# Moving TensorE's semaphore waits out of the 64x64 tile matmuls, onto full 128x128 products of the step before

## The chip, the cores and the metric

The kernel runs on one core of one Trainium2 chip. The metric is the time of one execution on the device in microseconds (us), the median of several runs. The core has five engines, each with its own instruction stream that runs in order: TensorE (PE, matmuls; its weight loads are shown apart as PEld), VectorE (DVE), ScalarE (ACT), GpSimd (POOL) and SyncE (SP, which issues the DMAs). The streams are tied to each other by semaphores: an instruction can wait until a semaphore that another engine raises has reached a value.

## The reference, cut to what matters

A layer norm, then two branches from its result: sliding-window attention with 32 heads of 20 columns and a window of 256 keys, and an MLP with a squared ReLU. The two are multiplied, with a SiLU on the MLP's side, and added to the input. S is 2048, D is 640, F is 1536.

```python
x = A_x
xn = _layernorm(x, axis=-1)
s = _A_ref(xn, A_wqkv, A_wo)
g = _silu(_B_ref(xn, B_w1, B_b1, B_w2, B_b2))
return x + s * g
```

`_A_ref` is `softmax(mask(q @ k.T * Dh**-0.5)) @ v`, the mask keeping keys 0 to 255 behind each query, followed by `@ wo`; `_B_ref` is `relu(xn @ w1 + b1)**2 @ w2 + b2`.

## The kernel before

All big products are done in float16 with operands split into a high and a low part, so one product in the reference becomes three on the chip. After a first part (layer norm, values, the first group of queries and keys, up to about 120 us of the profile) comes one long loop of 269 steps, the loop `for s in range(steps)` at L1023, in which attention and all the remaining dense products are interleaved by hand: the code is written in the order in which each engine is to run it, and no scheduler moves anything. A pair of heads (there are 16) takes 16 steps, one for each tile of 128 queries.

In step s, PE does this, in this order:

1. In every fourth step (s % 4 == 1) a transpose (`max_rows`, L584) of row maxima that POOL wrote to `mp`.
2. `scores` (L558): four matmuls into `sps`, each on a 64x64 quarter of the array, for the two heads of the pair. They are read by `maxima` on DVE (L569), which finds the row maxima. `sps` are two PSUM banks.
3. `scores_t` (L605): four more such quarter matmuls into `stps`, the transposed scores of ten steps earlier (LAG is 10), with the maxima already in two extra rows of `qs` (so in `scores_t` a wait for the small DMAs that bring those rows). `stps` is one tile. It is read by the exponential on ACT (`exps`, L610).
4. `fill` (L1007): full 128x128 products of the rest of the network, drawn from a generator in two portions, L1066 and L1075. Their lines are L689 (`mm_group`: queries and keys `qkps`, hidden units `hps`, and at the end `wops`) and L874 (`out_unit`, `yps`). Between the portions come the DVE and ACT parts that empty finished banks.
5. In every second step (s even, from 14 on) `values` (L638): 24 or fewer short full products into `ops` that multiply the exponentials of two query tiles with the values. In these steps the second portion of `fill` is 0.3 us smaller, in the others 0.3 us larger (SWING).

Steps with `values` are called value steps below, the others plain steps. Items 2 and 3 together are the "stretch of tiles": eight matmuls on quarters of the array, between full products on both sides. There are 266 such stretches: 256 steps have `scores`, and `scores_t` goes on for ten more.

On ACT the order in a step is: the exponential (L610), then the relu and square of a hidden unit if one is finished (L848, L849), then the float16 copy of the exponential of the step before (`high`, L618). DVE does the two maxima (L569), in every fourth step a copy of the transposed maxima (`mrow`, L588), the low part of an older exponential (L624), and what empties PSUM banks.

Who must wait for whom in a stretch: `scores` may overwrite `sps` only when DVE has read the maxima of the step before; `scores_t` may overwrite `stps` only when ACT has done the exponential of the step before; both need the DMAs that load `qs` and `ks`. These waits sit on the instruction that needs them, so inside the stretch.

Of the kernel before, what the change touches and what calls it, by code (L numbers as in the profile page):

```python
# [14 lines left out]
P = 128  # L15
# [42 lines left out]
def attn_mlp_kernel(ctx: ExitStack, tc, x, wqkv, wo, w1, b1, w2, b2, out):  # L58
# [485 lines left out]
        vps[p] = vp  # L544

    mts = {}

    def scores(p, q, between):
        i = p % 2
        r = [pat.tile([P, 4 * P], F32, tag="s", name="sps") for h in range(2)]  # L550
        rows = between and between(r[0])
        nk = min(WIN + HB, (q + 1) * P)
        for j in range(2):
            q0 = q * P + j * HB
            k0 = max(0, q0 - WIN)
            for h, ps in enumerate(r):
                rows_ = slice(HB * h, HB * h + HR)
                nc.tensor.matmul(ps[HB * j:HB * (j + 1), :nk], qs[i][rows_, q0:q0 + HB], ks[i][rows_, k0:k0 + nk], start=True, stop=True)  # L558
        return (r, mask if q > 1 else mask0[:, 2 * P - nk:], nk), rows

    def maxima(p, q, r):
        if q % 4 == 0:
            mts[p, q // 4] = mtp_.tile([P, 8], F32, tag="mt", name="mt")
        mt = mts[p, q // 4]
        r, mk, nk = r
        for h, ps in enumerate(r):
            junk = mtp_.tile([P, WIN + HB], BF16, tag="junk", name="junk")
            at_ = 4 * h + q % 4
            nc.vector.tensor_tensor_reduce(out=junk[:, :nk], in0=ps[:, :nk], in1=mk, scale=1.0 / MAX_UNIT, scalar=-3.0e38, op0=ALU.add, op1=ALU.max, accum_out=mt[:, at_:at_ + 1])  # L569
        if q % 4 == 3:  # L570
            mp = mps[q // 4 % 2]
            v = mp[:, 0:16].rearrange("p (h a b) -> p h a b", h=2, a=2)
            m_ = mt.rearrange("p (h b) -> p h b", h=2)
            nc.gpsimd.tensor_copy(v[:, :, 0, :], m_)  # L574
            nc.gpsimd.tensor_sub(v[:, :, 1, :], m_, v[:, :, 0, :])
            mts[p, q // 4] = mp

    def max_rows(p, g, tp=None):
        i = p % 2
        mp = mts.pop((p, g))  # L580
        if tp is None:
            tp = pat.tile([P, 4 * P], F32, tag="s", name="mtp")
        tp = tp[:, 3 * P:3 * P + P // 2].bitcast(F16)
        nc.tensor.transpose(tp, mp, identh)  # L584

        def rest():
            mrow = mtp_.tile([16, P], F16, tag="mrow", name="mrow")
            nc.vector.tensor_copy(mrow, tp[0:16, :])  # L588
            for h in range(2):
                post(qs[i][HB * h + HR:HB * h + ER, 4 * P * g:4 * P * (g + 1)].rearrange("a (b n) -> a b n", n=P), mrow[8 * h:8 * (h + 1), :])  # L590
        return rest

    pts = {}
    ots = {}
    sts = []

    def scores_t(p, kb):
        i = p % 2
# [8 lines left out]

    def exps(p, kb, ps, n):
        p32 = at2.tile([P, 2, 3 * P], F32, tag="p32", bufs=3, name="p32")
        nc.scalar.activation(p32[:, :, :n], ps[:, :, :n], AF.Exp, scale=esc[0], bias=ebias)  # L610
# [50 lines left out]
    state = [0.0, 0.0, 0]  # L661
    posts = []

    def post(dst, src):
        posts.append((dst, src))

    def post_all():
        for dst, src in posts:
            nc.sync.dma_start(dst, src)
        posts.clear()  # L670

    pending, late = [], []
# [5 lines left out]
    def flush(upto=None):  # L678
# [3 lines left out]
        while pending and (upto is None or flushed[0] < upto):  # L682
            flushed[0] += 1
            pending.pop(0)()

    def mm_group(ps, mms, cost):
        n = len(mms)
        for j, (a, b_) in enumerate(mms):
            nc.tensor.matmul(ps, a, b_, start=j == 0, stop=j == n - 1)  # L689
            yield cost  # L690


    bulk = []
# [8 lines left out]
            fn()  # L702
            credit[0] -= cost

    def bulk_dma(cost, dst, src):
        item = (cost, lambda: nc.sync.dma_start(dst, src))
        bulk.append(item)
        return item

# [148 lines left out]
    def out_unit(n, tt, nh, third):  # L858
        if (n, tt, nh, third) == (0, 0, 0, 0):
            for j in range(3):  # L860
                ensure(f"2{j}")
        t = n * 2 + tt
        sl = slice(nh * HALF, (nh + 1) * HALF)
        fs = range(third * THIRD, (third + 1) * THIRD)
        flush(ready_h[n, fs[-1]])
        if third == 0:
            if nh == 0:
                outs[t] = wgt.tile([P, D], F32, tag="ysb", name="ysb")
            outs[t, nh] = pmm.tile([P, HALF], F32, tag="mm", name="yps")
        ps, ysb = outs[t, nh], outs[t]  # L870
        for fc in fs:
            hh = hidden[n, fc // 2][:, fc % 2]
            for j, (hp, wp) in enumerate(((0, 0), (0, 1), (1, 0))):
                nc.tensor.matmul(ps, hh[:, hp, tt * P:(tt + 1) * P], lin1(w2t, (2 * fc + wp) * D + nh * HALF, HALF), start=fc == 0 and j == 0, stop=fc == NF - 1 and j == 2)  # L874
                yield 0.138

        def evac():
            nc.vector.scalar_tensor_tensor(ysb[:, sl], ps, mlp["i2"], b2t[:, sl], ALU.mult, ALU.add)
# [138 lines left out]
    with tc.manual_schedule(engines={E_.PE, E_.Activation, E_.DVE, E_.Pool, E_.SP}):  # L1017
# [5 lines left out]
        for s in range(steps):  # L1023
            state[2] = s
            post_all()
            issue(RATE)
            a, b, c, d, e = (at_step(s - lag) for lag in (0, LAG, LAG + 1, LAG + 2, LAG + 3))
            if a:
                p, q = a
                if q == 0:  # L1030
                    ensure_bulk(loads)
                if s == 2:
                    ones_rows(1)
                if s == 3:
                    nc.scalar.activation(early, eps, AF.Exp)
                    sts.append(pst.tile([P, 2, 4 * P], F32, tag="st", name="stps"))
                    nc.vector.memset(sts[0][:, :, 0:3 * P], 0.0)
                if s == 5:
                    load_v(0)
                if q == 2 and p < NP - 1:  # L1040
                    loads = [bulk_dma(0.7, *l) for l in pair_loads(p + 1, 0)]
                if q == LAG and p < NP - 1:
                    loads += [bulk_dma(0.7, *l) for l in pair_loads(p + 1, 1)]
                if q == LAG + 4 and p < NP - 1:
                    load_v(p + 1)
            rows = between = None
            if s % 4 == 1 and 1 < s <= NP * NT + 1:
                def between(tp=None, s=s):
                    return max_rows((s - 2) // NT, (s - 2) % NT // 4, tp)
# [62 lines left out]
```

## Time and profile before

| | |
|---|---|
| median of 3 runs | 838.02 us (837.1 to 838.42) |
| the profiled execution's own time | 837.25 us |
| its span, first to last instruction | 835.5 us |
| busy: PE, DVE, ACT, POOL | 98%, 82%, 78%, 57% of the span |
| mean granted clock of PE | 0.998 of full speed |
| the loop with stretches of tiles | about 120 to 750 us of the span |

How to read the rows shown below. A row of the timeline has the start in us from the span's start, the length in us, engine, source line, operation, output and inputs, shapes, how many equal ones that follow each other are merged (x8), and in brackets the idle time of the engine ahead of it with what ended it. Matmuls overlap in the pipeline: a product of 128x320 is listed with a length of 0.30 us, but the next one starts 0.136 us later. A row of the groups has the count, the busy time in all, the mean length of one in ns, and the idle time ahead. A row of the windows has, for each engine, the busy time within the stretch of time named at its start.

### The profile page before, as it was taken

Reading aid. Unit: us, or ns where it says so; the run is one execution under the profiler, and the core shown is the slowest. Engines: PE = TensorE matmul, PEld = TensorE weight load, DVE = VectorE, ACT = ScalarE, POOL = GpSimd, SP = SyncE. Lnnn points to the kernel's source line nnn. Section 1 sums busy time; section 2 is a strip of 40 time slices with the busy share of each in tenths; the row PEclk is TensorE's granted clock in tenths of the full one; section 3 lists DMA queues with packets and bytes.
Section 4 is the critical chain, followed back from the end, with each engine's and each line's share of the span. In section 5 each row is a group of like instructions: output and inputs, shape, how many; then the busy total and the mean of one; then the engine's idle time right before and its main releaser. Section 6 shows DMA issues by size and latency. Waiting matters only on the chain.

```text
span 835.5 us, 24908 instructions
## 1 busy us (share of the span) xinstructions
PE 815.3 (98%) x9426; PEld 548.1 (66%) x9426; DVE 686.0 (82%) x1897; ACT 648.5 (78%) x1028; POOL 476.9 (57%) x874
## 2 busy tenths in 40 slices
PE   8999999999989999999999999999999999999998
PEld 6765563445545557777777777777777777767775
DVE  6777576788999889888988889888988889875665
ACT  5456455998898989898898989898898989893321
POOL 2000001446777768797878878797887878770000
PEclk9999999999999999999999999999999999999999
DMA  6894447765463332212121212211121131055873
GB/s 240 253 342 123 146 147 255 232 183 158 145 197 119 100 102 79 52 49 66 50 68 58 67 49 54 56 60 50 54 89 45 55 97 46 10 199 181 309 288 129
DMA packets 100497, 104.51 MB, mean 125 GB/s; under 512 B 42520, under 2 KB 72856, under 8 KB 100376
## 3 DMA queue, kind: packets, MB, share of 16 engines
q1 hardware_dynamic: 100376, 102.91, 39.5%
q8 instruction: 74, 1.21, 0.6%
q14 instruction: 47, 0.39, 0.2%
HBM read 65.67 MB, written 36.83 MB: 123 GB/s over the span
## 4 chain that ended last, share of the span: by engine, by line
PE 82%; ACT 7%; DVE 5%; issue 3%; DMA 2%; SPq 0%; DVEq 0%; ACTq 0%
PE hps L689 19%; PE yps L874 19%; PE wops L689 8%; PE ops L638 7%; PE vps L292 7%; PE sps L558 7%; PE qkps L689 7%; PE stps L605 3%; PE qkps L503 3%; ACT p L610 2%; DVE junk L569 2%; ACT ph L618 1%; PE otp L956 1%; PE tps L256 1%; DVE pl L624 1%
## 5 line engine op out<-in xcount | busy, mean ns | idle before, releaser
L610 ACT ACTIVATE p<-stps,ebias,esc 128x768 f32<-128x768 f32 (+2 forms) x256 | 242.3, 947 | 50.2 <-PE stps L605 42.4
L569 DVE CUSTOM_DVE_ANT_0 junk<-sps,mask 128x320 bf16<-128x320 f32 (+2 forms) x512 | 221.3, 469 | 54.8 <-PE sps L558 44.6
L624 DVE TENSOR_TENSOR pl<-p,ph 128x768 f16<-128x768 f32 (+2 forms) x256 | 243.6, 952 | 4.7 <-ACT ph L618 4.0
L611 POOL TENSOR_SCALAR_AFFINE_SELECT p<-p 128x256 f32<-128x256 f32 x256 | 171.4, 670 | 90.4 <-ACT p L610 87.8
L618 ACT ACTIVATE ph<-p 128x768 f16<-128x768 f32 (+2 forms) x256 | 203.2, 794 | 1.9 <-POOL p L613 0.9
L689 PE MATMUL hps<-xT,w 128*128 128x256 f16 x1440 | 188.8, 273 | 0.0
L874 PE MATMUL yps<-w,hh 128*128 128x320 f16 x1152 | 186.6, 300 | 0.0
L689 PEld LDWEIGHTS <-w 128*128 128x128 f16 x1440 | 133.3, 98 | 43.7 <-issue 23.7
L874 PEld LDWEIGHTS <-hh 128*128 128x128 f16 x1152 | 105.1, 98 | 55.6 <-issue 21.8
L689 PE MATMUL qkps<-xT,qkw 128*128 128x512 f16 x480 | 117.0, 381 | 0.8 <-DVE w_t L153 0.8
L613 POOL TENSOR_SCALAR_AFFINE_SELECT p<-p 128x256 f32<-128x256 f32 x224 | 110.5, 493 | 0.0
L558 PE MATMUL sps<-ks,qs 60*64 60x320 f16 (+2 forms) x1024 | 86.1, 313 | 6.5 <-DVE mt L569 5.9
L638 PE MATMUL ops<-vp,ph 128*128 128x41 f16 x1440 | 89.8, 181 | 0.0
L638 PE MATMUL ops<-vp,pl 128*128 128x41 f16 x1440 | 89.5, 181 | 0.0
L638 PEld LDWEIGHTS <-ph 128*128 128x128 f16 x1440 | 84.6, 96 | 6.2 <-issue 0.6
L638 PEld LDWEIGHTS <-pl 128*128 128x128 f16 x1440 | 78.9, 96 | 5.8
L605 PE MATMUL stps<-qs,ks 62*64 62x320 f16 (+4 forms) x1024 | 79.6, 291 | 2.3 <-ACT p L610 2.0
L574 POOL CAST mp<-mt 128x8 f16<-128x8 f32 x64 | 44.1, 689 | 62.2 <-DVE mt L569 61.6
L689 PEld LDWEIGHTS <-qkw 128*128 128x128 f16 x480 | 41.6, 98 | 53.4 <-issue 11.7
L852 POOL TENSOR_TENSOR hh<-sq,hh 128x256 f16<-128x256 f32 x96 | 67.6, 704 | 13.0 <-DVE sq L851 9.3
L292 PE MATMUL vps<-wv,xT 128*128 128x320 f16 x480 | 70.0, 302 | 3.2 <-ACT xT L261 1.6
L689 PE MATMUL wops<-wo,oT 128*128 128x320 f16 x480 | 66.7, 299 | 0.8 <-ACT oT L121 0.8
(150 smaller groups left out, 974.8 us busy)
## 6 DMA issues: line engine op xcount, KB each, us to landing
ks<-k_d SPq DMA_DIRECT2D x64, 120.0 KB
qs<-q_d SPq DMA_DIRECT2D x64, 120.0 KB
raw<-in_B_w_dram SPq DMA_DIRECT2D x24, 320.0 KB
v_d<-vt SPq DMA_DIRECT2D x8, 656.0 KB
vp<-v_d SPq DMA_DIRECT2D x16, 328.0 KB
xt<-in_A_x_dram SPq DMA_DIRECT2D x16, 320.0 KB
k_d<-shm SPq DMA_DIRECT2D x20, 256.0 KB
q_d<-shm SPq DMA_DIRECT2D x20, 256.0 KB
```

Source lines behind the costliest of these rows:

```text
L292: nc.tensor.matmul(ps, xT[b][:, xp, c, t * P:(t + 1) * P], wv[wp][:, c, nh * HALF:(nh + 1) * HALF], start=n == 0, stop=n == 3 * KC - 1)
L558: nc.tensor.matmul(ps[HB * j:HB * (j + 1), :nk], qs[i][rows_, q0:q0 + HB], ks[i][rows_, k0:k0 + nk], start=True, stop=True)
L569: nc.vector.tensor_tensor_reduce(out=junk[:, :nk], in0=ps[:, :nk], in1=mk, scale=1.0 / MAX_UNIT, scalar=-3.0e38, op0=ALU.add, op1=ALU.max, ...
L605: nc.tensor.matmul(ps[HB * j:HB * (j + 1), hh, c0:c1], ks[i][rows_, kb * P + HB * j:kb * P + HB * (j + 1)], qs[i][rows_, kb * P + c0:kb * ...
L610: nc.scalar.activation(p32[:, :, :n], ps[:, :, :n], AF.Exp, scale=esc[0], bias=ebias)
L611: nc.gpsimd.affine_select(p32[:, :, 0:P], p32[:, :, 0:P], pattern=[[0, 2], [1, P]], compare_op=ALU.is_ge, fill=0.0, base=0, channel_multip ...
L613: nc.gpsimd.affine_select(p32[:, :, 2 * P:], p32[:, :, 2 * P:], pattern=[[0, 2], [-1, P]], compare_op=ALU.is_gt, fill=0.0, base=0, channel ...
L618: nc.scalar.activation(ph[:, :, :n], p32[:, :, :n], AF.Copy)
L624: nc.vector.tensor_sub(pl[:, :, :n], p32[:, :, :n], ph[:, :, :n])
L638: nc.tensor.matmul(ot[:, q % 4, hh, :], t[:, hh, (q - k) * P:(q - k + 1) * P], vp[:, k // 4, k % 4, hh, :], start=m == 1, stop=m == 2 * le ...
L689: nc.tensor.matmul(ps, a, b_, start=j == 0, stop=j == n - 1)
L874: nc.tensor.matmul(ps, hh[:, hp, tt * P:(tt + 1) * P], lin1(w2t, (2 * fc + wp) * D + nh * HALF, HALF), start=fc == 0 and j == 0, stop=fc = ...
```

## The change

The scores' two PSUM banks and the bank of the sums are made once (`sps`, `opst`) rather than asked of the pool in each step. Each instruction that reads a bank of a stretch (the last of the two maxima, the `mrow` copy, the exponential), and each POOL write or DMA that the next stretch needs, is noted in a list `users`. At the end of the fill of step s, ahead of `values`, `wait_ahead` gives the last full products of that step a wait for them, one each, from the last product backwards: the last product waits for the maxima of this step, the one before it for `mrow` in the steps that have one, the next for this step's exponential, and those before for POOL writes and DMAs that the next step needs. A wait that PE has already done isn't repeated, so the stretch of the next step has none left. DMAs are issued by the new helper `send` in the same order.

```diff
     def scores(p, q, between):
         i = p % 2
-        r = [pat.tile([P, 4 * P], F32, tag="s", name="sps") for h in range(2)]
-        rows = between and between(r[0])
+        if not sps:
+            sps.extend(pat.tile([P, 4 * P], F32, tag="s", name="sps") for h in range(2))
+        r = sps
+        rows = between and between()
...
+            read = nc.vector.tensor_tensor_reduce(out=junk[:, :nk], in0=ps[:, :nk], in1=mk, scale=1.0 / MAX_UNIT, scalar=-3.0e38, op0=ALU.add, op1=ALU.max, accum_out=mt[:, at_:at_ + 1])
+        users.append(read)
...
+            landing.append((p * NT + q + 2, nc.gpsimd.tensor_sub(v[:, :, 1, :], m_, v[:, :, 0, :])))
...
+            users.append(nc.vector.tensor_copy(mrow, tp[0:16, :]))
...
-        nc.scalar.activation(p32[:, :, :n], ps[:, :, :n], AF.Exp, scale=esc[0], bias=ebias)
+        users.append(nc.scalar.activation(p32[:, :, :n], ps[:, :, :n], AF.Exp, scale=esc[0], bias=ebias))
...
-            ots[p, q // 4] = po_.tile([P, 4, 2, VW], F32, tag="o", name="ops")
+            if not opst:
+                opst.append(po_.tile([P, 4, 2, VW], F32, tag="o", name="ops"))
+            ots[p, q // 4] = opst[0]
...
+    def send(dst, src, due=0):
+        dma = nc.sync.dma_start(dst, src)
+        if due:
+            landing.append((due, dma))
...
+    dense = []
+
     def mm_group(ps, mms, cost):
         n = len(mms)
         for j, (a, b_) in enumerate(mms):
-            nc.tensor.matmul(ps, a, b_, start=j == 0, stop=j == n - 1)
+            dense.append(nc.tensor.matmul(ps, a, b_, start=j == 0, stop=j == n - 1))
             yield cost
+
+    def wait_ahead(s):
+        for item in landing[:]:
+            if item[0] <= s + 1:
+                users.append(item[1])
+                landing.remove(item)
+        for mm, user in zip(reversed(dense), users):
+            tc.add_manual_dep(mm.ins, user.ins.name, mybir.DependencyInfo(mybir.DependencyClass.Sync, mybir.DependencyReason.DATA))
+        dense.clear()
+        users.clear()
...
             fill((1 - EARLY_FILL) * per + SWING * (-1) ** (s - LAG - 3))
+            wait_ahead(s)
             if e and e[1] % 2:
                 values(e[0], e[1] - 1)
```

The order of instructions is the same on all five engines; only PE's waits differ. Two places of PE's stream show it, both around step 116, a value step (its stretch starts at 401.86 us in the profile of before). Names in brackets are the semaphores waited for: DVE and Activation are raised by those engines, DMAHW by landing DMAs, Pool by POOL.

The first place is the stretch itself. Before, on PE, from its first weight load on:

```order
L558 LDWEIGHTS qs1_1562
L558 MATMUL sps_7388<-ks1_1563,qs1_1562 64x320 [waits DVE_49]
L558 LDWEIGHTS qs1_1562
L558 MATMUL sps_7389<-ks1_1563,qs1_1562 64x320 [waits DVE_49]
L558 LDWEIGHTS qs1_1562
L558 MATMUL sps_7388<-ks1_1563,qs1_1562 64x320
L558 LDWEIGHTS qs1_1562
L558 MATMUL sps_7389<-ks1_1563,qs1_1562 64x320
L605 LDWEIGHTS ks0_127 [waits DMAHW7_49]
L605 MATMUL stps_1647<-qs0_126,ks0_127 64x320 [waits Activation_49]
```

Now, on PE, the last four full products ahead of the same stretch, and its first load:

```order
L896 LDWEIGHTS hh_6169 [waits DMAHW0_49]
L896 MATMUL yps_6911<-w2_2_3779,hh_6169 128x320
L896 LDWEIGHTS hh_6169 [waits DMAHW7_49]
L896 MATMUL yps_6911<-w2_2_3779,hh_6169 128x320
L896 LDWEIGHTS hh_6169 [waits Activation_49]
L896 MATMUL yps_6911<-w2_2_3779,hh_6169 128x320
L896 LDWEIGHTS hh_6169 [waits DVE_49]
L896 MATMUL yps_6911<-w2_2_3779,hh_6169 128x320
L561 LDWEIGHTS qs1_1562
```

All waits of the stretch now stand on the weight loads of the four products ahead of it (L874 has become L896, L558 has become L561), and the eight quarter matmuls have none.

The second place is the end of step 116, where its full products end and `values` begins. Before, on PE:

```order
L874 LDWEIGHTS hh_6609
L874 MATMUL yps_7157<-w2_2_3887,hh_6609 128x320
L689 LDWEIGHTS w1_0_1320
L689 MATMUL hps_7425<-xT_1_499,w1_0_1320 128x256
L689 LDWEIGHTS w1_0_1320
L689 MATMUL hps_7425<-xT_1_499,w1_0_1320 128x256
L638 LDWEIGHTS ph_7151
```

Now, on PE, the same rows:

```order
L896 LDWEIGHTS hh_6386 [waits Pool_49]
L896 MATMUL yps_6911<-w2_2_3779,hh_6386 128x320
L701 LDWEIGHTS w1_0_1320 [waits Activation_49]
L701 MATMUL hps_7168<-xT_1_499,w1_0_1320 128x256
L701 LDWEIGHTS w1_0_1320 [waits DVE_49]
L701 MATMUL hps_7168<-xT_1_499,w1_0_1320 128x256
L643 LDWEIGHTS ph_6905
```

Nothing has moved but the waits: the one for ACT (this step's exponential) is now on the second-to-last product, ahead of `values`; before, it was on the first `stps` matmul of the next stretch, behind `values`.

More of the change, by code (lines that the diff above doesn't have):

```diff
@@ L703, in issue, with bulk_dma @@
             credit[0] -= cost
-    def bulk_dma(cost, dst, src):
-        item = (cost, lambda: nc.sync.dma_start(dst, src))
+    def bulk_dma(cost, dst, src, due):
+        item = (cost, lambda: send(dst, src, due))
         bulk.append(item)
@@ L873, in out_unit @@
             for j, (hp, wp) in enumerate(((0, 0), (0, 1), (1, 0))):
-                nc.tensor.matmul(ps, hh[:, hp, tt * P:(tt + 1) * P], lin1(w2t, (2 * fc + wp) * D + nh * HALF, HALF), start=fc == 0 and j == 0, stop=fc == NF - 1 and j == 2)
+                dense.append(nc.tensor.matmul(ps, hh[:, hp, tt * P:(tt + 1) * P], lin1(w2t, (2 * fc + wp) * D + nh * HALF, HALF), start=fc == 0 and j == 0, stop=fc == NF - 1 and j == 2))
                 yield 0.138
@@ L1040, in attn_mlp_kernel @@
                 if q == 2 and p < NP - 1:
-                    loads = [bulk_dma(0.7, *l) for l in pair_loads(p + 1, 0)]
+                    loads = [bulk_dma(0.7, *l, (p + 1) * NT) for l in pair_loads(p + 1, 0)]
                 if q == LAG and p < NP - 1:
-                    loads += [bulk_dma(0.7, *l) for l in pair_loads(p + 1, 1)]
+                    loads += [bulk_dma(0.7, *l, (p + 1) * NT + NT // 2) for l in pair_loads(p + 1, 1)]
                 if q == LAG + 4 and p < NP - 1:
@@ L1047, in attn_mlp_kernel, with between @@
             if s % 4 == 1 and 1 < s <= NP * NT + 1:
-                def between(tp=None, s=s):
-                    return max_rows((s - 2) // NT, (s - 2) % NT // 4, tp)
+                def between(s=s):
+                    return max_rows((s - 2) // NT, (s - 2) % NT // 4)
             if a:
```

23 lines of the change are left out of this document (10 added, 13 removed).

## Prediction

> **What bounds the kernel now.** I read the page's busy times first, then the busy time by stretches of time, then PE's waits, then the timeline of single steps.
>
> ```profile
> PE 815.3 (98%) x9426; PEld 548.1 (66%) x9426; DVE 686.0 (82%) x1897; ACT 648.5 (78%) x1028; POOL 476.9 (57%) x874
> ```
>
> ```profile
> core 0: us, PE busy (x) PEld busy (x) DVE busy (x) ACT busy (x) POOL busy (x), PEclk, DMA share, GB/s
> 126.00:262.00 136.00, 126.56 (x1314) 64.41 (x1313) 118.49 (x336) 118.43 (x189) 76.27 (x145) 1.00 0.62 190
> 262.00:300.00 38.00, 38.00 (x460) 21.34 (x459) 33.70 (x101) 33.40 (x51) 27.16 (x53) 1.00 0.37 108
> 300.00:727.00 427.00, 427.00 (x5883) 305.05 (x5881) 380.48 (x1120) 383.24 (x585) 345.45 (x609) 1.00 0.21 59
> 727.00:760.00 33.00, 31.85 (x402) 22.86 (x400) 23.36 (x36) 27.25 (x39) 19.85 (x31) 1.00 0.46 151
> ```
>
> PE is busy 427.00 of 427 us from 300 to 727 us: there it never waits, at full clock, and whatever delays PE by some time lengthens the kernel by it. ACT is next, 383.24 of 427 (90%). From 126 to 262 us PE is idle for 136 - 126.56 = 9.4 us. These are the waits that the change can take out of the stretches:
>
> ```profile
> PE sps L558 <- DVE mt L569: 5.9, 10, 1.1
> PE stps L605 <- ACT p L610: 2.0, 5, 0.9
> ```
>
> So 7.9 us in 15 stretches are real waits, all but one ahead of 300 us (from there to 727 us PE has no idle time). In the other 250 or so the wait is already met when PE comes to it.
>
> **What a wait costs that is already met.** Here is a stretch of step 116, and the start of the one of step 117:
>
> ```profile
> 401.63 0.30 PE L874 MATMUL yps<-w,hh 128*128 128x320 f16 x1
> 401.86 0.33 PE L558 MATMUL sps<-ks,qs 60*64 60x320 f16 x4
> 402.02 0.31 PE L605 MATMUL stps<-qs,ks 62*64 62x320 f16 x4
> ...
> 402.26 1.26 PE L874 MATMUL yps<-w,hh 128*128 128x320 f16 x8
> 403.36 0.38 PE L689 MATMUL hps<-xT,w 128*128 128x256 f16 x2
> ```
>
> ```profile
> 404.18 0.22 PE L584 MATMUL sps<-identh,mp 128*128 128x128 f16 x1
> 404.33 0.33 PE L558 MATMUL sps<-ks,qs 60*64 60x320 f16 x4
> ```
>
> Full products of 320 columns follow each other every (1.26 - 0.30) / 7 = 0.137 us, those of 256 every 0.38 - 0.27 = 0.11. Going into the stretch takes 401.86 - 401.63 = 0.23, so 0.09 more than a product does. Going out takes 402.26 - 402.03 = 0.23, again 0.09 more. The first product behind a stretch has no wait, yet costs the same 0.09. The transpose of step 117 has 128 columns, by the two spacings above about 0.055 us; 404.33 - 404.18 = 0.15 is again 0.09 more, and the `sps` matmul behind it has no wait either (its bank's wait stands on the transpose). So the 0.09 at both ends belongs to the change from full products to quarters and back, not to the waits, and a met wait costs nothing that I can read. Gain from the 250 stretches without a real wait: 0. The Trainium skill, page "TensorEngine Tiling (Array Packing)", section "Key Properties", says that changing the tiling mode drains TensorE; by that rule too the two edges stay whatever the waits do, and the trace agrees with its 0.09 at an edge without a wait.
>
> **What a wait costs on a full product.** The loop of before has no full product whose load came late, but the kernel's first part has some:
>
> ```profile
> 37.53 0.84 PE L292 MATMUL vps<-wv,xT 128*128 128x320 f16 x5
> ...
> 37.92 0.25 PEld L292 LDWEIGHTS <-xT 128*128 128x128 f16 x3 [0.15 <-ACT xT L261]
> ```
>
> ```profile
> 38.50 0.81 DVE L266 TENSOR_TENSOR xT<-tps,xT 128x640 f16<-128x640 f32 x1
> 39.02 0.93 PE L292 MATMUL vps<-wv,xT 128*128 128x320 f16 x5
> ...
> 39.37 0.39 PEld L292 LDWEIGHTS <-xT 128*128 128x128 f16 x4 [0.24 <-DVE xT L266]
> ```
>
> Five products take 0.84 us with a load that came 0.15 after the one before it had ended, and 0.93 where it came 0.24 after. The spacing in the first, (0.84 - 0.30) / 4 = 0.135, is the undisturbed one, so that late load cost nothing: a weight load runs a whole product ahead, and only what is later than its product's own turn delays PE. In the second, a load usually begins 0.04 after the one before it has ended, so this one was 0.20 late, and 0.09 of that was lost. The release took 39.37 - (38.50 + 0.81) = 0.05 to 0.06 us. So the price of a moved wait is: end of the instruction waited for, plus 0.05, minus the time at which the product would have started anyway.
>
> **Part one, the wait for the exponential (the term that counts).** `scores_t` of step s is followed by this step's exponential, and the change makes PE wait for it at the second-to-last full product of the same step (third-to-last where there is an `mrow`), no longer at the next `scores_t`. In a value step `values` lies between the two places, 24 products. Step 116, whose products are above, has on ACT:
>
> ```profile
> 402.38 0.99 ACT L610 ACTIVATE p<-stps,ebias,esc 128x768 f32<-128x768 f32 x1 [0.32 <-PE stps L605]
> ```
>
> ACT was idle for 0.32 and started as early as it can, 0.36 after the last `stps` matmul. The exponential ends at 403.37, released 403.42. The second-to-last product is the first of the two `hps`, at 403.36. Late by 0.06. That is the mild kind, and ACT cannot do better. The other kind is a value step in which ACT comes late, since a relu and its square lay between the last exponential and this one:
>
> ```profile
> 360.17 1.37 PE L689 MATMUL hps<-xT,w 128*128 128x256 f16 x11
> 360.42 0.97 ACT L610 ACTIVATE p<-stps,ebias,esc 128x768 f32<-128x768 f32 x1
> ```
>
> The exponential ends at 361.39, released 361.44. The last of the eleven products starts at 360.17 + 1.37 - 0.27 = 361.27, the one before at 361.16. Late by 0.28.
>
> I did this subtraction for each of the 183 exponentials from 300 to 727 us, carrying each delay on (each exponential starts at the later of two times, 0.36 after its delayed `stps` or when ACT is free; a delayed PE gives ACT time to catch up):
>
> ```profile
> L610 ACT ACTIVATE p<-stps,ebias,esc 128x768 f32<-128x768 f32 (+2 forms) x183 | 172.5, 943 | 38.0 <-PE stps L605 34.5 <-DVE shm L81 0.9 <-DVE ysb L878 0.8
> ```
>
> Of the 92 value steps, 57 have no relu just ahead of the exponential: 0.15 each in the mean, 8.4 us. 35 have one: 0.29 each, 10.1 us. The 91 plain steps have 0.6 us more of full products (SWING twice) and add 0.8 us in all. Sum **19.3 us**. As PE has no idle time there, all of it is on the path, and nothing hides it.
>
> From 262 to 300 us the same sum over 15 steps gives **2.5 us**. From 727 to 760 there are eleven exponentials without `scores`; at 0.2 for each of five value steps, **1 us**.
>
> **Part two, 126 to 262 us.** Here PE already waits in the stretches, as in step 46:
>
> ```profile
> 231.93 0.46 PE L558 MATMUL sps<-ks,qs 60*64 60x320 f16 x4 [0.36 <-DVE mt L569]
> 232.07 0.46 PE L605 MATMUL stps<-qs,ks 62*64 62x320 f16 x4
> ```
>
> `sps` took 0.46 there instead of 0.33: when the first quarter waits, the four don't start together, and 0.13 is lost on top. That goes when the wait is met earlier, at most 0.13 to 0.4 in 15 stretches, 2 to 4 us. The wait itself doesn't go: it is moved ahead by two products and, in value steps, by `values`, and DVE and ACT are busy for 118 of 136 us. Lower end: -3 us. Upper end: each of the 46 exponentials here costs what the worse kind costs above, 46 x 0.28 = 13. I take the mean of 92 value steps above, 18.5 / 92 = 0.20, for the 23 value steps here: **5 us**, nearest to the rows that I could work out.
>
> **Part three, the other waits.** The wait for the maxima is on the last product. The maxima are awaited at the last product, the DMAs that bring the extra rows of `qs` two steps after their issue:
>
> ```profile
> 403.06 0.08 DVE L569 DVE_READ_ACCUMULATOR2_ANT mt<- 128x1 f32 x1
> ```
>
> ```profile
> 405.76 1.28 SPq L669 DMA_DIRECT2D qs<-mrow  x2
> ```
>
> ```profile
> 406.90:407.90 1.00, 1.00 (x15) 0.62 (x8) 1.00 (x4) 0.72 (x2) 0.91 (x3) 1.00 0.02 4
> ```
>
> In step 116 the second maximum has ended at 403.14, and the last product starts at 403.47: 0.3 to spare; its cover is the first portion of full products, and without it a step would lose as much as DVE is behind (90% busy, so 0 to 0.3). I take 0. The two DMAs issued at 405.76 carry 4 KB, and 4 GB/s for 1 us is 4 KB: they have moved by 407.9, and are awaited near the end of step 119, past 410.5. The POOL writes to `mp` are awaited a step after they were issued. The fixed banks change no instruction and no order, on SP's and POOL's queues either. All 0.
>
> **The sum**, against the profiled execution's own 837.25 us: 19.3 + 2.5 + 1 + 5 = 27.8, so **865 us**. That execution is 0.1% below the median of the runs, 838.02, so the two give the same to a microsecond.
>
> **The rivals.**
>
> *The waits are what makes the edges dear.* If a met wait kept PE from loading the quarters ahead, and the product behind them too, 0.09 at each end of 266 stretches would go, 48 us, and with the 27.8 for the moved waits it would be 837 - 48 + 28 = 817 us, faster. It decides for faster from 28 / 266 = 0.105 us saved per stretch on. Against it are the two edges without a wait and the same 0.09. Chance 5%.
>
> *Nothing to be measured.* The moved waits cost only where PE waits anyway, and the 7.9 us of waits pay for the rest: 837 us. It needs the exponential to be ready when PE comes to the product; in step 116 it is not, with ACT idle ahead of it. Chance 5%.
>
> *Dearer.* The load that holds the wait is the point that counts, with no product's time of allowance (0.11 to 0.14 more in each late step): the same carried sum is then 29 us from 300 to 727, 4 from 262 to 300, and with 13 ahead of it and 2 behind 48 us, 885 us. The five products at 37.53 speak against it. Chance 10%.
>
> **How the numbers follow.** The forecast, some 20 to 40 us slower, has 80%; its own bounds are -3 and +13 for part two, and a third of the 22 us of part one either way (0.05 us per step in the release, the start of ACT or the product's place): 849 to 881. Dearer reaches to 885. Low 849, high 882 leaves out both small cases and the top of the dear one, under 2 in 10. Slower by over 0.2% (1.7 us, about what a measurement of this kernel can tell from no change): 90%; within it 5%; faster 5%.
>
> **What would show it.** In the profile of the changed kernel, from 300 to 727 us PE should have idle gaps of 0.1 to 0.4 us ahead of the weight loads of L701 and L896, put down to ACT p, in most value steps and few plain ones; the stretch from 401 us on should come some 12 to 16 us later than now; the edges of the stretches should still be 0.23 us from start to start; the waits of PE for L558 and L608 should be gone. A pair of steps should take 4.9 us where it takes 4.7. I'd be wrong if the edges fall below 0.2 us, or if PE stays without gaps from 300 us on because ACT starts the exponential sooner than 0.36 us after `stps`.

## The result, and the profile after

The changed kernel takes **870.74 us** (median of six runs, 868.78 to 871.11), beside 837.56 us (836.2 to 839.05, six runs) for the kernel before on the same chip: a ratio of 1.0389, 95% interval 1.0377 to 1.04. The forecast was 865 us, 849 to 882. The profiled execution of the changed kernel has a span of 869.2 us and a mean granted clock of 0.994.

The page's busy times, and the busy time by stretches of time, of the changed kernel (columns: time, length, then PE, PEld, DVE, ACT and POOL busy, granted clock of PE, DMA share, GB/s):

```profile
PE 834.4 (96%) x9426; PEld 531.8 (61%) x9426; DVE 684.2 (79%) x1897; ACT 652.1 (75%) x1028; POOL 475.5 (55%) x874
```

```profile
126.00:262.00 136.00, 121.06 (x1225) 54.32 (x1229) 109.35 (x311) 111.92 (x177) 71.35 (x135) 0.97 0.62 185
262.00:300.00 38.00, 35.67 (x414) 18.33 (x411) 31.86 (x93) 31.53 (x47) 24.29 (x46) 1.00 0.35 94
300.00:727.00 427.00, 419.94 (x5584) 280.32 (x5582) 360.97 (x1067) 366.78 (x557) 327.34 (x580) 1.00 0.22 60
727.00:760.00 33.00, 32.67 (x431) 21.98 (x429) 28.54 (x86) 28.28 (x44) 25.09 (x46) 1.00 0.07 20
```

From 300 to 727 us PE was busy for 427.00 of 427 us; now it is 419.94, and gets 5584 matmuls done there where it did 5883. The idle time of 7.06 us is much less than the loss: a product is listed with its whole way through the pipeline, 0.30 us, while the next one follows 0.137 us later, so a product that comes up to 0.16 us late doesn't show as idle time at all. What PE and its weight loads wait for (columns: us in total, times, the longest) tells more:

```profile
PE qkps L701 <- ACT p L613: 9.7, 24, 1.1
PE qkps L701 <- DMA qs<-mrow: 3.7, 1, 3.7
PE yps L896 <- ACT p L613: 2.3, 8, 0.7
PE hps L701 <- ACT p L613: 2.3, 10, 0.4
```

No row of the stretch's own lines, L561 and L608, is left among PE's waits. The four rows shown stand on full products, and all but the second are for the exponential. The smaller rows of the same list add 2.6 us in seven waits for the maxima and `mrow`, all of them ahead of 300 us.

Because the order of instructions is the same in both kernels, each matmul can be set beside the same matmul of the other trace. The table gives how much later it comes than before, by where the time arises (the columns are stretches of the trace of before, in us; the rows below the change are the experiments of the next section). The forecast's 5 us for 126 to 262 us stand behind 140 us, since the first exponential starts at 141.3 us.

| | median us | 126–140 | 140–262 | 262–300 | 300–727 | behind 727 | sum |
|---|---|---|---|---|---|---|---|
| forecast | 865 | 0 | 5 | 2.5 | 19.3 | 1 | 27.8 |
| the change | 870.74 | 5.6 | 4.4 | 3.4 | 20.5 | 0.6 | 34.4 |
| e1_exp_back | 844.0 | 3.0 | 1.6 | 0.9 | 0.3 | 0.0 | 5.8 |
| e2_exp_only | 867.0 | 0.7 | 4.7 | 2.9 | 20.4 | 0.6 | 29.2 |
| e3_rows_later | 868.06 | 0.8 | 5.7 | 3.4 | 20.6 | 0.6 | 31.1 |
| e4_after_values | 849.73 | 4.5 | 1.7 | 1.5 | 3.5 | 0.3 | 11.4 |
| e5_banks | 837.1 | 1.0 | -0.7 | 0.0 | 0.0 | 0.2 | 0.4 |
| e6_exp_last | 857.96 | 5.8 | 3.4 | 2.4 | 10.2 | 0.6 | 22.4 |
| e7_exp_early | 952.1 | 4.5 | 25.7 | 10.6 | 71.4 | 2.9 | 115.0 |
| e9_all_last | 841.83 | 1.0 | 2.8 | 0.5 | 0.1 | 0.3 | 4.7 |
| e10_last_from20 | 839.09 | 1.1 | 0.7 | 0.5 | 0.1 | 0.2 | 2.6 |

The sums differ from those of the spans by what lies ahead of 126 us, where the kernels are alike (between -1.1 and 2.1 us from one execution to the next). So a microsecond in the columns ahead of 300 us is little; the column from 300 to 727 us is the sharp one. The medians are of all runs, the columns of the profiled execution alone, and the two can be some us apart: e4_after_values was profiled at 847.59 us, e6_exp_last at 861.75 us.

**The stretch of step 116 again.** PE's rows of the changed kernel, its weight load, and ACT's exponential:

```profile
419.92 0.57 PE L896 MATMUL yps<-w,hh 128*128 128x320 f16 x3
420.42 0.33 PE L561 MATMUL sps<-ks,qs 60*64 60x320 f16 x4
420.58 0.31 PE L608 MATMUL stps<-qs,ks 62*64 62x320 f16 x4
420.82 1.26 PE L896 MATMUL yps<-w,hh 128*128 128x320 f16 x8
421.99 0.39 PE L701 MATMUL hps<-xT,w 128*128 128x256 f16 x2
```

```profile
421.99 0.11 PEld L701 LDWEIGHTS <-w 128*128 128x128 f16 x2 [0.24 <-ACT p L613]
```

```profile
420.94 0.99 ACT L613 ACTIVATE p<-stps,ebias,esc 128x768 f32<-128x768 f32 x1 [0.60 <-PE stps L608]
```

The stretch comes at 420.42 instead of 401.86. Its edges are what they were: the last product ahead of it starts at 419.92 + 0.57 - 0.30 = 420.19, 0.23 before the first quarter, and the first product behind it 0.24 after the `stps` row starts, as before (402.02 to 402.26). The exponential ends at 421.93, and the load that waits for it begins at 421.99. Before, the same `hps` product came 1.10 us after the first `yps` of the row above it (402.26 to 403.36), now 1.17: 0.07 lost, where the forecast had 0.06.

The dear kind of step, in which ACT has a relu and its square to do first:

```profile
366.82 1.16 PE L701 MATMUL hps<-xT,w 128*128 128x256 f16 x9
368.26 0.45 PE L896 MATMUL yps<-w,hh 128*128 128x320 f16 x2 [0.28 <-ACT p L613]
```

```profile
368.25 0.11 PEld L896 LDWEIGHTS <-hh 128*128 128x128 f16 x2 [0.56 <-ACT p L613]
```

```profile
365.58 0.56 ACT L870 ACTIVATE relu<-hps,m,m 128x256 f32<-128x256 f32 x1
366.17 0.42 ACT L871 ACTIVATE hh<-relu 128x256 f16<-128x256 f32 x1
366.49 0.83 ACT L621 ACTIVATE ph<-p 128x768 f16<-128x768 f32 x1
367.23 0.97 ACT L613 ACTIVATE p<-stps,ebias,esc 128x768 f32<-128x768 f32 x1
```

The last of the nine products starts at 366.82 + 1.16 - 0.27 = 367.71, so the `yps` behind it was due at 367.82. It comes at 368.26, 0.44 late, behind an exponential that ended at 368.20. Of these 0.44 PE's row shows 0.28 as idle, and the load's row 0.56, since a load is due one product ahead.

### The profile page after: what moved, and what is told of

It is laid out like the page before. It is cut to its first block, busy times and chain, and to the rows that moved or that the text cites. A ratio compares the mean times of both kernels' runs of the same rounds, so it can differ in the third digit from the quotient of the medians.

```text
span 869.2 us, 24891 instructions
## 1 busy us (share of the span) xinstructions
PE 834.4 (96%) x9426; PEld 531.8 (61%) x9426; DVE 684.2 (79%) x1897; ACT 652.1 (75%) x1028; POOL 475.5 (55%) x874
## 4 chain that ended last, share of the span: by engine, by line
PE 57%; ACT 17%; issue 5%; DVE 4%; DMA 1%; SPq 0%; POOL 0%; ACTq 0%; DVEq 0%
PE yps L896 14%; PE hps L701 14%; ACT p L613 10%; PE ops L643 8%; PE wops L701 8%; PE sps L561 6%; PE qkps L701 4%; PE stps L608 3%; ACT ph L621 3%; ACT relu L870 2%; DVE junk L572 1%; DVE pl L627 1%; PE otp L978 1%; ACT hh L871 1%; ACT shm L80 1%
## 5 line engine op out<-in xcount | busy, mean ns | idle before, releaser
L613 ACT ACTIVATE p<-stps,ebias,esc 128x768 f32<-128x768 f32 (+2 forms) x256 | 242.5, 947 | 73.5 <-PE stps L608 67.3
L627 DVE TENSOR_TENSOR pl<-p,ph 128x768 f16<-128x768 f32 (+2 forms) x256 | 238.9, 933 | 3.6 <-ACT ph L621 2.9
L614 POOL TENSOR_SCALAR_AFFINE_SELECT p<-p 128x256 f32<-128x256 f32 x256 | 172.2, 673 | 100.7 <-ACT p L613 96.6
L701 PE MATMUL hps<-xT,w 128*128 128x256 f16 x1440 | 196.2, 274 | 4.9 <-ACT p L613 2.3
L896 PE MATMUL yps<-w,hh 128*128 128x320 f16 x1152 | 193.4, 300 | 3.8 <-ACT p L613 2.3
L701 PEld LDWEIGHTS <-w 128*128 128x128 f16 x1440 | 129.3, 98 | 61.0 <-issue 23.7
L896 PEld LDWEIGHTS <-hh 128*128 128x128 f16 x1152 | 100.8, 98 | 71.9 <-issue 21.8
L701 PE MATMUL qkps<-xT,qkw 128*128 128x512 f16 x480 | 126.1, 386 | 16.5 <-ACT p L613 9.7
L701 PEld LDWEIGHTS <-qkw 128*128 128x128 f16 x480 | 39.5, 98 | 83.8 <-ACT p L613 28.3
L561 PE MATMUL sps<-ks,qs 60*64 60x320 f16 (+2 forms) x1024 | 83.1, 314 | 0.0
L874 POOL TENSOR_TENSOR hh<-sq,hh 128x256 f16<-128x256 f32 x96 | 69.1, 720 | 14.7 <-DVE sq L873 10.5
L608 PE MATMUL stps<-qs,ks 62*64 62x320 f16 (+4 forms) x1024 | 77.1, 290 | 0.0
L701 PE MATMUL wops<-wo,oT 128*128 128x320 f16 x480 | 66.7, 299 | 0.8 <-ACT oT L121 0.8
```

Of the source, the lines that this page charges most:

```text
L608: nc.tensor.matmul(ps[HB * j:HB * (j + 1), hh, c0:c1], ks[i][rows_, kb * P + HB * j:kb * P + HB * (j + 1)], qs[i][rows_, kb * P + c0:kb * ...
L613: users.append(nc.scalar.activation(p32[:, :, :n], ps[:, :, :n], AF.Exp, scale=esc[0], bias=ebias))
L627: nc.vector.tensor_sub(pl[:, :, :n], p32[:, :, :n], ph[:, :, :n])
L701: dense.append(nc.tensor.matmul(ps, a, b_, start=j == 0, stop=j == n - 1))
L896: dense.append(nc.tensor.matmul(ps, hh[:, hp, tt * P:(tt + 1) * P], lin1(w2t, (2 * fc + wp) * D + nh * HALF, HALF), start=fc == 0 and j == ...
```

## The experiments

All edits are against the changed kernel unless said. Lines move by a few from kernel to kernel: L702 below is L701, L899 is L896, L614 is L613. An entry `None` in `users` holds its place in the list, but adds no wait.

**e1_exp_back: only the exponential's wait goes back into the stretch.**

```diff
-        users.append(nc.scalar.activation(p32[:, :, :n], ps[:, :, :n], AF.Exp, scale=esc[0], bias=ebias))
+        nc.scalar.activation(p32[:, :, :n], ps[:, :, :n], AF.Exp, scale=esc[0], bias=ebias)
+        users.append(None)
...
         for mm, user in zip(reversed(dense), users):
+            if user is None:
+                continue
```

> The change without its wait for the exponential on a full product: that wait goes back to the next stretch (stps, L608); the waits for maxima, mrow, POOL and DMAs stay on the full products. If the loss is the exponential's wait ahead of values (theory): the 20.5 us of 300 to 727 us, the 3.4 of 262 to 300 and the 0.6 of 727 to 760 go, and of the 10 us between 126 and 262 the 4 to 6 stay that come from the wait for the first mrow DMA: 840 to 846 us, 843 in the middle. If any met wait on a full product costs something by itself (rival one: 520 DVE and DMA waits stay there, about 280 go): 858 to 862. If the loss lies with the other moved waits (rival two): 866 to 871, as the change.

Measured: 844.0 us (842.86 to 846.57), ratio 1.0082, interval 1.006 to 1.0104. Busy times from 300 to 727 us:

```profile
300.00:727.00 427.00, 426.85 (x5869) 303.19 (x5866) 380.45 (x1119) 383.52 (x584) 345.58 (x609) 1.00 0.22 60
```

PE is full again, with 5869 matmuls for before's 5883, although some 500 moved waits for DVE, POOL and DMAs (over the whole loop) still stand on full products. So a met wait on a full product costs nothing that shows either, and the other moved waits carry almost none of the loss behind 300 us (0.3 us). Of the 5.8 us that stay, 5.5 lie ahead of it. PE waits there for the first small DMAs, and for the maxima and `mrow`, mainly in these two rows:

```profile
PE qkps L702 <- DVE mt L572: 8.3, 11, 1.3
PE qkps L702 <- DMA qs<-mrow: 3.0, 1, 3.0
```

Before, PE waited for the maxima 10 times ahead of 300 us, for 5.9 us in all. So ahead of 300 us the moved waits for the maxima aren't all met, and cost something too: from 140 to 300 us e1_exp_back loses 1.6 + 0.9 = 2.5 us.

**e2_exp_only: the exponential's wait alone is moved.** The other entries of `users` become `None`, and `landing` isn't read.

```diff
-        users.append(read)
+        users.append(None)
...
-            users.append(nc.vector.tensor_copy(mrow, tp[0:16, :]))
+            nc.vector.tensor_copy(mrow, tp[0:16, :])
+            users.append(None)
...
-        for item in landing[:]:
-            if item[0] <= s + 1:
-                users.append(item[1])
-                landing.remove(item)
```

> The change with the exponential's wait alone moved, to the same product as in the change (second-to-last, third-to-last with an mrow); the waits for maxima, mrow, POOL and DMAs stay in the stretch and ahead of the transpose, as before. Theory: the whole of the loss behind 160 us is there, only the wait for the first mrow DMA near 138 us is gone: 20 to 21 us between 300 and 727 us as in the change, and 864 to 867 us in all. Rival: the loss needs the other moved waits too (they hold PE, so ACT comes late): under 860.

Measured: 867.0 us (865.58 to 868.2), ratio 1.0345, interval 1.0331 to 1.036. From 300 to 727 us 20.4 us arise, as in the change (20.5). e1 and e2 are the two halves of the change, and from 262 us on the table's columns add up: 0.9 and 2.9 are 3.8 for 3.4, and 0.3 and 20.4 are 20.7 for 20.5. From 140 to 262 us they don't (1.6 and 4.7 are 6.3 for 4.4).

**e6_exp_last: one product more for ACT.** In the list of waits the exponential (`exp_user[0]`) takes the last product, and the maxima the one ahead of it.

```diff
+        users.sort(key=lambda u: u is not exp_user[0])
         for mm, user in zip(reversed(dense), users):
```

> The change, with the exponential's wait on the last full product of the fill and the maxima's one product ahead of it: one product (0.11 or 0.137 us) more of time for ACT in each step. If the price is the exponential's end plus 0.05 minus the product's own start (theory): each of 92 late value steps between 300 and 727 us, 0.22 us late in the mean, is up to 0.12 less late, so 8 to 11 us less there, 1 to 2 in 262 to 300, 1 to 3 in 126 to 262: 855 to 861 us, 858 in the middle. If the loss is a fixed price of a wait that has a gap (rival): 869 to 872, as the change; if the maxima's wait one product earlier costs as much as the exponential's gains (another rival): over 862, with DVE mt as what L701 and L896 wait for.

Measured: 857.96 us (856.71 to 861.75), ratio 1.0239, interval 1.0222 to 1.0257. The loss from 300 to 727 us falls from 20.5 to 10.2, by 10.3 where 8 to 11 were expected. The maxima, one product earlier, are awaited only once from 300 us on (0.3 us).

**e7_exp_early: four products less for ACT.** Four empty places are put into the list ahead of the exponential.

```diff
+        users.extend([None] * 4)
         users.append(nc.scalar.activation(p32[:, :, :n], ps[:, :, :n], AF.Exp, scale=esc[0], bias=ebias))
```

> The change with the exponential's wait four products further ahead (sixth-to-last, seventh-to-last with an mrow), so 0.44 to 0.55 us less time for ACT in each step. By the carried sum (the exponential's end plus 0.05 minus the product's own start, each delay handed on) 70.8 us are lost between 300 and 727 us where the change loses 20.5, and 38.8 before 300: 837.4 + 112 and 3 for the early DMA, 953 us, 935 to 965. Rival (the loss is a price per wait and not the time the exponential lacks): 868 to 876, as the change.

Measured: 952.1 us (951.43 to 952.88), ratio 1.1364, interval 1.1347 to 1.1381. PE's waits over the whole kernel:

```profile
PE qkps L702 <- ACT p L614: 38.8, 48, 1.4
PE yps L899 <- ACT p L614: 26.1, 49, 1.2
PE hps L702 <- ACT p L614: 25.9, 56, 0.8
```

From 300 to 727 us 71.4 us are lost, where the sum gave 70.8. The same wait, in the same form and number, costs 10, 20 and 71 us at three places: its price is the time that the exponential lacks, not the wait.

**e4_after_values: in value steps the exponential is awaited behind `values`.** The wait stays on a full product, and out of the stretch. `exp_users` holds this step's exponential, `ahead` adds one wait, and `values` returns its last product.

```diff
-            wait_ahead(s)
-            if e and e[1] % 2:
+            vals = e and e[1] % 2
+            users.extend([None] if vals else exp_users)
+            wait_ahead(s)
+            if vals:
                 values(e[0], e[1] - 1)
-                values(*e)
+                last = values(*e)
+                for user in exp_users:
+                    ahead(last, user)
```

> The change, with the wait for the exponential of a value step on the last product of values instead of the second-to-last product of the fill (in plain steps as in the change). No wait goes back into a stretch. If what costs is the place, ahead of values (theory): of 20.5 us between 300 and 727 us about 1 stays, of 3.4 before it 0.5, and of the 10 us from 126 to 262 some 5 to 7 stay: 843 to 848 us, 845 in the middle. If a wait on the load of a full product costs by its form, wherever it stands (rival): 866 to 871, as the change.

Measured: 849.73 us (847.59 to 851.64), ratio 1.0145, interval 1.0124 to 1.0167. The place was what cost: from 300 to 727 us 3.5 us are left of 20.5. The median is 1.7 above the range expected, though the profiled execution, 847.59, is inside it. From 126 to 262 us 6.2 stay, as expected (5 to 7): the early wait for the DMA is still there, with a stretch at half clock behind it. Behind that there is more than was expected, 1.5 for 0.5 and 3.5 for 1. Of the 3.5, the plain steps lose 3.2, where in the change they lose 0.4: in the change a delay in a value step lets ACT catch up, and in the mean over the plain steps its exponential starts 0.45 us after the last `stps` matmul; in e4_after_values it is 0.54, as before. The other three runs, 848.96 to 851.64 us, have a lower granted clock (0.991 to 0.993, where the profiled one has 0.995).

**e3_rows_later: the first DMA rows of each pair are awaited two steps later.**

```diff
-                post(qs[i][HB * h + HR:HB * h + ER, 4 * P * g:4 * P * (g + 1)].rearrange("a (b n) -> a b n", n=P), mrow[8 * h:8 * (h + 1), :], p * NT + 4 * g + LAG - 2)
+                post(qs[i][HB * h + HR:HB * h + ER, 4 * P * g:4 * P * (g + 1)].rearrange("a (b n) -> a b n", n=P), mrow[8 * h:8 * (h + 1), :], p * NT + 4 * g + LAG - 2 * (g > 0))
```

> The change, with one number different: the DMAs that bring the extra rows of qs for the first four tiles of a pair are awaited in the step ahead of their use, two steps later than in the change (all waits still stand on full products). If the 3.8 us wait for the first of them at 137.6 us and the half clock of 6.8 us behind it cost time that nothing gives back (theory): PE has no wait for that DMA near 138 us, the granted clock stays above 0.95 from 135 to 145 us, and the time falls by 3 to 6 us to 865 to 868. If the lost time is waited for anyway (rival: DVE and ACT lag behind PE in the steps that follow, so their waits take up what this one leaves): 869.5 to 871.

Measured: 868.06 us (867.31 to 868.17), ratio 1.0363, interval 1.0348 to 1.0379, 0.06 us above the range expected; the interval just touches the change's own (from 1.0377). Here is what the edit takes away, in the changed kernel: SP's issues, PE and its load.

```profile
133.31 1.30 SPq L670 DMA_DIRECT2D qs<-mrow  x2
```

```profile
132.68 1.25 PE L701 MATMUL qkps<-xT,qkw 128*128 128x512 f16 x5
137.61 1.46 PE L701 MATMUL qkps<-xT,qkw 128*128 128x512 f16 x3 [3.67 <-DMA qs<-mrow]
```

```profile
137.60 0.13 PEld L701 LDWEIGHTS <-qkw 128*128 128x128 f16 x2 [4.17 <-DMA qs<-mrow]
```

The small DMAs are issued from 133.31 on, when PE is in step 7 already (its stretch starts at 132.42), and the end of step 7 waits for them, though `scores_t` reads the rows in step 10 only. They have landed at 137.6, 4.3 us after the first was issued: the queues are full of weights (342 GB/s from 135 to 140 us). PE stands still for 3.67 us, and the clock halves. The windows of 135 to 140 and 140 to 145 us, first of the change, then of e3_rows_later:

```profile
135.00:140.00 5.00, 2.39 (x9) 0.70 (x10) 0.38 (x1) 0.97 (x4) 0.00 (x0) 0.58 1.01 342
140.00:145.00 5.00, 5.00 (x28) 1.70 (x25) 2.26 (x10) 2.14 (x5) 0.00 (x0) 0.73 0.61 191
```

```profile
135.00:140.00 5.00, 3.88 (x23) 1.38 (x24) 2.54 (x10) 2.18 (x6) 0.00 (x0) 1.00 1.04 358
140.00:145.00 5.00, 3.58 (x28) 1.12 (x27) 2.26 (x8) 4.08 (x9) 0.77 (x2) 1.00 0.87 271
```

From 126 to 140 us 4.8 us are saved (0.8 for 5.6), and the half clock is gone; 1.3 come back from 140 to 262 us (5.7 for 4.4), where ACT and DVE are awaited instead. That leaves 3.3 us by the sums of the table, and 2.7 by the medians.

**e5_banks: the kernel before, with banks that are made once and nothing else.** Its diff is the lines on `sps` and `opst` of the change.

> The kernel before, with the two banks of the scores and the bank of the sums made once, and no other edit; all waits stay where they were. Theory (fixed banks cost and bring nothing, the instructions and their order are the same): 836.5 to 838.5 us, PE busy 427 of 427 us from 300 to 727 us. Rival (a bank that is not asked for anew loses a release that ran ahead, and adds waits): over 839.

Measured: 837.1 us (836.31 to 838.72), ratio 0.9993, interval 0.9984 to 1.0001. PE is busy for 427.00 of 427 us. The fixed banks cost and bring nothing.

**e9_all_last: all waits out of the stretch, but as late as a full product allows.** As e6_exp_last and e3_rows_later together, and in value steps the waits stand on the last products of `values` (listed in `vals`).

```diff
-        for mm, user in zip(reversed(dense), users):
+        users.sort(key=lambda u: u is not exp_user[0])
+        for mm, user in zip(reversed(dense + vals), users):
...
-            wait_ahead(s)
             if e and e[1] % 2:
                 values(e[0], e[1] - 1)
                 values(*e)
                 if e[1] % 4 == 3:
                     norm.append(normed(e[0], e[1] // 4))
+            wait_ahead(s)
```

> All waits stay out of the stretch, but stand as late as a full product allows: in value steps on the last products of values, in plain steps on the last of the fill, the exponential's on the very last and the maxima's one ahead; the first rows' DMAs two steps later as in e3_rows_later. Theory (no wait costs by itself, only the time that it comes too early): by the carried sum 0.1 us is lost between 300 and 727 us and 2.5 before it: 838.5 to 842 us, 840 in the middle. If waits inside a stretch did cost something of their own, it would be gained here: under 836. If a wait on a full product costs by its form: over 850.

Measured: 841.83 us (840.51 to 842.49), ratio 1.0044, interval 1.0031 to 1.0056. Its busy times:

```profile
300.00:727.00 427.00, 427.00 (x5868) 303.85 (x5866) 380.83 (x1121) 383.32 (x585) 343.99 (x608) 1.00 0.22 60
```

This is what the change set out to do, at no cost from 300 to 727 us (0.1 us): 182 stretches free of waits, and not a microsecond gained.

**e10_last_from20: the same from step 20 on only.**

```diff
-            wait_ahead(s)
+            if s < 20:
+                users.clear(), dense.clear(), vals.clear()
+            else:
+                wait_ahead(s)
```

> As e9_all_last (all waits on the last full product ahead of the next stretch, those of values in value steps), but only from step 20 on (166 us of the trace before); the first 20 steps have their waits where they were before. Theory (what e9_all_last still lost lies between 126 and 165 us, where the weights' loads fill the DMA queues and a wait put ahead holds PE for them; behind that a wait placed this late costs nothing, and taking waits out of a stretch brings nothing): 836.5 to 839 us, within 0.2% of before. Rival (taking the waits out of the 250 stretches does bring something, hidden so far by the early loss): under 835.5. Rival (waits on full products cost something later too): over 840.

Measured: 839.09 us (838.16 to 840.95), ratio 1.0019, interval 1.001 to 1.0029. That is 2.1 us above its own runs of before (837.01), and 0.09 above the range expected. By the traces 2.3 us arise ahead of 300 us, where e5_banks, with the waits of before, has 0.3, and 0.1 from there to 727 us. No kernel tried is faster than the one before by more than its measurement can tell, and e9_all_last and e10_last_from20, with their waits out of the stretches, are slower by 0.4% and 0.2%.

## Why the prediction held, and where it was off

- **What bounds the kernel** (right). PE was full from 300 to 727 us, so each delay there lengthened the kernel: 20.5 us arise there and none of it is given back later.
- **The edges don't belong to the waits** (right). They are 0.23 us with all waits gone, and e9_all_last has 182 stretches without waits at 0.1 us of difference. The edge behind a stretch is 0.23 us in before, the change and e9_all_last alike, in the median of the 182, 174 and 182 stretches from 300 to 727 us. The rival of 817 us fell.
- **Price of a moved wait** (right). "End of the instruction waited for, plus 0.05, minus the time at which the product would have started anyway" gave 0.06 for step 116, measured 0.07, and with the wait at three places it met all three: 20.5 us for 19.3 in the change, 71.4 for 70.8 four products earlier, and 10.3 less than the change for 8 to 11 less one product later.
- **Part one** (right). From 300 to 727 us 19.3 us were forecast, 18.5 of it in value steps and 0.8 in plain ones. By the two traces, taking the places at which PE falls behind by more than 0.012 us, it is 19.2 us at 90 places in value steps and 0.3 at 7 places in plain ones; the rest of the 20.5 is smaller pieces. By kind of step the forecast holds too: the value steps without a relu just ahead of the exponential lose 9.7 us (8.4 forecast), those with one 10.3 (10.1). From 262 to 300 us it is 3.4 for 2.5, behind 727 us 0.6 for 1.
- **Part two** (near, in part by luck). 5 us were taken, with bounds of -3 and 13; from 140 to 262 us 4.4 arise, and 4.7 and 5.7 in e2_exp_only and e3_rows_later. But the 5 was the mean of steps in which PE is always full, carried over to steps in which it isn't; moved waits for the maxima that aren't met fall into the same column, and in e2_exp_only a stretch at half clock (141.8 to 145.2 us), neither of which the forecast has. The 2 to 4 us that were to be gained where the quarters don't start together aren't seen: e9_all_last, with no wait in a stretch there, is 2.8 us later from 140 to 262 us.
- **Part three** (wrong ahead of 300 us). "All 0" was read at step 116, where two such DMAs landed within 2.1 us of their issue on queues with 4 GB/s. The first two go out from 133.31 us on into queues with 342 GB/s and have landed 4.3 us later, and the change awaits them three steps ahead of their use. This one wait, with the half clock that came with it, is most of the 5.6 us from 126 to 140 us; e3_rows_later takes away 4.8 of them there. Of the miss in the sum, 34.4 - 27.8 = 6.6 us, 5.6 are here; from 300 to 727 us it is 1.2 more than forecast and from 262 to 300 us 0.9, the rest 1.0 less. The 0.9 is the second place at which "all 0" failed. PE's waits in the changed kernel from 262 to 300 us:

```profile
PE qkps L701 <- ACT p L613: 1.0, 4, 0.3
PE qkps L701 <- DVE mt L572: 1.0, 2, 0.6
```

In the same stretch e1_exp_back, which moves the waits for the maxima but not those for the exponential, loses 0.9 us. Step 116 had 0.3 us to spare for the maxima; DVE is later than that in two of these steps. The stretch at 401.86, forecast 12 to 16 us later, came 18.6 later, mostly for the wait at 137.6 us.
- **The dearer rival** (no product of allowance, 885 us) fell. It had 29 us from 300 to 727 us, where 20.5 arise. Who waited for the exponential from 312.6 to 760.1 us of the changed kernel, which is 300 to 727 of before (columns: idle us, times):

```profile
  PEld L896: 18.0, 52
  PEld L701: 16.1, 46
```

PE's loads were idle for 34.1 us ahead of these 98, of which some 0.03 each is the usual gap between two loads (0.01 to 0.04). Set beside before, each load comes 0.32 us later behind the product ahead of it, in the mean, and its own product only 0.20. The difference of 0.12 is one product's spacing (0.11 to 0.137): a load runs one product ahead, and that much lateness is free. What the profile was to show was there, but for the place of the stretch at 401.86: gaps of that size ahead of the loads of L701 and L896, in the value steps, and 4.91 us for a pair of steps, in the mean over the 174 stretches from 300 to 727 us, where before it was 4.68 over 182.

## What to carry to other kernels

A wait that is already met cost nothing here at any place tried (in the stretch, on full products, on `values`), so moving it ahead couldn't gain; it could only be moved from where it is met to where it isn't. Before a wait is moved up in an in-order stream, list what lies between the two places (here 24 products of `values`, which had covered the exponential) and subtract, step by step, the end of what is awaited from the start of the instruction that is to wait. For DMAs take the latency from the busiest stretch in which the wait occurs, not from a quiet one.

## What the hardware did that was not expected

The granted clock of PE halved in the changed kernel during its longest wait (half clock from 135.8 to 142.7 us, the wait's end at 137.6), though PE had been busy for 0.44 of the window of the clock ahead of that. The clock's records have lengths that are multiples of 3.41 us, and these are windows of that length, two of e2_exp_only and two of e5_banks; the clock is the third number from the end of a row:

```profile
138.34:141.75 3.41, 1.44 (x12) 0.45 (x11) 2.19 (x10) 2.41 (x6) 0.00 (x0) 1.00 0.99 324
141.75:145.16 3.41, 3.34 (x15) 0.92 (x16) 1.60 (x5) 2.79 (x7) 1.55 (x6) 0.50 0.95 311
```

```profile
138.30:141.70 3.40, 1.60 (x14) 0.65 (x13) 2.54 (x10) 2.12 (x6) 0.00 (x0) 1.00 1.04 331
141.70:145.10 3.40, 3.38 (x28) 1.30 (x27) 1.80 (x6) 3.40 (x8) 1.49 (x6) 1.00 0.91 300
```

A window in which PE was busy for 1.44 of 3.41 us (0.42) was followed by one at half clock; one with 1.60 of 3.40 (0.47) was not. The longest gap of PE doesn't decide it: it is 1.84 us in e2_exp_only and 2.11 in e5_banks. In all eleven traces, from 60 to 830 us, half clock followed each window in which PE was busy for 0.44 or less (five of them), and no full-clock window with 0.47 or more. The Trainium skill, page "TensorE: Matmul & The Clock Gate", section "Part 1: The HAM clock gate", says that the clock is halved after at least one idle window of about 3.4 us. The length of the window agrees with the records; but the window needn't be idle here: windows that the trace shows as busy for 0.23 to 0.44 were enough.
